# Low parts of two units on other engines, and routing work regrouped, in an attention and two-MoE kernel

## The chip, the cores and the metric

The kernel runs on one core of one Trainium2 chip, in one launch. The metric is the device time in microseconds (us), as a median of runs. A profiled execution gives the rows below; its times are us from the start of the span, unless they are marked ns. PE is the matrix engine (TensorE), PEld its weight loads, DVE is VectorE, ACT is ScalarE, POOL is GpSimd, SP is SyncE, which mostly issues DMAs (SPq and ACTq are DMA issues on those engines' queues).

## The reference, cut to what matters

```
def attn(q, k, v, centroids):          # B=2, H=8, S=768, D=64, 16 centroids a head
    q_assign = argmax(norm(q) @ norm(centroids).T); k_assign = the same of k
    scores = where(q_assign == k_assign, q @ k.T / sqrt(D), -1e9)
    return softmax(scores) @ v
def moe(x, w_gate, w1, w2, capacity):  # x 1536 x 512, 8 experts, hidden 1024, capacity 384
    e = argmax(x @ w_gate); gate = softmax(x @ w_gate)[e]
    keep the first `capacity` tokens of each expert, in order
    out[token] = gate * (relu(x @ w1[e]) @ w2[e])      # zero where not kept
def moe2(x, w_gate, w_output_gate, w1, w2):            # no capacity
    out[token] = gate * sigmoid(x @ w_output_gate)[e] * (relu(x @ w1[e]) @ w2[e])
return moe2(moe(attn(...)))
```

The output of the attention is the input of the first MoE (stage 1), whose output is the input of the second (stage 2). Each token has one expert per stage, so the rows of a stage are sorted by expert.

## The kernel before

**Attention.** The 16 heads of 768 rows are worked in 8 head pairs with 96 score tiles of 128 x 768 (`pss` L238, its row maximum `nm` L246 on DVE, exponential `pe` L254 on ACT, transposes `ppt` L268, product with v `av` L280). `norm` multiplies by the gate weights as well (`px` L299), so that the gate logits `lp` of stage 1 come with the output; `after_half` then chooses experts for each half (three tiles of 128 rows, C = 6 tiles in a batch of 768). At the start, centroids are loaded and normalised (`cl`, `cw` L355, `c_n` L66 to L68), logits against them give two masks of five steps each (`first_mask`, L207 to L217, to the transposes `poh` L223), and `first_rows(0)` builds the first operands. Matmuls on a zero tile (`keep_warm`, `warm_up`, L26) run in TensorE's idle time at the start.

**Experts.** A unit is a block of rows of one expert. Stage 1 has units 0 to 8 of 128, 64, 304, 208, 200, 192, 176, 168 and 120 rows, stage 2 has units 9 to 16 of 256, 136, 272, 120, 224, 128, 192, 160 and more; 0 and 9 are the heads, and open their expert without closing it. Every product is made of three f16 products of high and low parts. `mm1` works through eight f-steps of 12 matmuls (`ph` L930), after each of which ACT writes the high part `hh` (L932) and DVE the low part `hl` (L933). `mm2` follows with four d-steps (`py` L996, eight high, eight low-weight and eight `hl` matmuls each), or `pz` L971 by token, as in unit 9. `xg` is a block of gathered rows, transposed (`pxt` L907) and split into `xh` (ACT, L908) and `xl` (DVE, L909). Weights come as raw f32 by SP, and are split into `wh` (L820, ACT) and `wl` (L827, DVE) in half chunks.

**Handovers.** A stage's rows go to DRAM (x1d, x2d) once their experts and positions are known, and are read back by gathers on POOL (L867, `xg<-x2d,idx`), which need the indices `idx` from a DVE chain: choose the expert, count positions with a matmul (`ppos` L1522 in the attention, L1718 to L1721 in the second handover), scale the row (L1447 ACT, L1449 POOL; L1711 POOL), gates (L1753, L1755), invert the permutation (`av`, `rv` L587 to L595, matmul L600) and look up (L646, L649). At the end of stage 1 the outputs `yt` are first transposed back (`pyo` L1609), with logits `pq` (L1637, L1645; copy `lt` L1640) and a flag product (`flt`, `okr`, L1013, L1015), and scaled to `xo` (L1661, L1662). Groups of units (`group1`) are routed together.

**What sets the order.** Each engine's queue runs in program order, and waits on semaphores. `run()` writes the order by tables: `PIECES` gives a unit's weight splits per step, `SA` and `SB` the background steps per f- or d-step of the two heads (a background step is one `next` on the routing generators), `FX`, `FB`, `FY` the f-step at which the previous unit's `exit` starts. Where a routing generator yields, other work is placed. The last attention pair's second half, `last()`, is a background task of unit 0. The head's gather and entry stand as follows:

```
                if d == 1 and self.ngather == i + 2:
                    self.gather()
                if d == 3 and self.nmeta == i + 2:
                    self.meta()
            if head:
                assert nxt.gt, "unit not gathered"
                for k in range(len(nxt.tiles)):
                    self.entry(nxt, k)
```

## Time and profile before

| | before |
|---|---|
| median of 3 runs | 629.47 us (627.88 to 630.0) |
| the profiled execution | 627.58 us |
| its span | 625.7 us |
| mean granted TensorE clock | 0.976 |
| PE / PEld busy | 569.5 / 470.8 us |
| DVE / ACT / POOL busy | 467.1 / 419.9 / 212.8 us |
| DMA moved | 117.55 MB, mean 188 GB/s |

The profiled execution is 627.58 - 625.7 = 1.9 us longer than its span. A busy share says how much an engine worked, not that it set the end; the chain of waits and the idle time before an instruction say which engine another one waited for. The granted clock is the share of TensorE's full speed that it had: at 1.00 it ran at 2.4 GHz, at 0.50 at 1.2 GHz. In a timeline row the first number is the start, the second the length (of all of a row's instructions where it ends in x2 or more), and the brackets give the idle time of that engine ahead of the row and what ended it.

### The profile page before, as it was taken

The page shows a single profiled execution, that of the slowest core. Times are in us where ns is not written, and L with a number is a line of the kernel's source. Part 1 is how long each engine was busy: PE and PEld are TensorE (multiplying, and loading weights), DVE is VectorE, ACT ScalarE, POOL GpSimd, SP SyncE. Part 2 cuts the span into 40 slices and gives each one's busy share as a digit, 9 for nine tenths or more (in the row PEclk, how much of TensorE's full clock was granted, in tenths as well). Part 3 has the DMA queues.
Part 4 walks back from the last instruction along what each step waited for, and adds up shares of the span by engine and source line. Part 5 has one row for each costly group of instructions (what it writes and reads, how often), then busy time and mean ns, then how long its engine had stood idle before and what let it go on. Part 6 is the DMA issues. An engine that isn't in the chain of part 4 may idle for free.

```text
span 625.7 us, 14519 instructions
## 1 busy us (share of the span) xinstructions
PE 569.5 (91%) x5430; PEld 470.8 (75%) x5430; DVE 467.1 (75%) x1219; ACT 419.9 (67%) x885; POOL 212.8 (34%) x420
## 2 busy tenths in 40 slices
PE   6899999998999988958999998998788899999992
PEld 2766767675767666637878997997767888999992
DVE  5767777679899677756597689788776566989881
ACT  4766666776666669832676776876654466979781
POOL 8702020204150210134615268344333623253341
PEclk9899999999999999998899999999899799999998
DMA  5779391826429952314486776977754457998930
GB/s 148 212 231 275 97 216 46 210 60 151 141 89 233 252 171 82 133 56 138 130 269 204 243 244 179 304 238 244 248 181 152 164 174 238 305 308 298 321 111 20
DMA packets 75518, 117.55 MB, mean 188 GB/s; under 512 B 10504, under 2 KB 43400, under 8 KB 75441
## 3 DMA queue, kind: packets, MB, share of 16 engines
q1 hardware_dynamic: 71585, 105.96, 56.1%
q0 software_dynamic: 3264, 9.72, 4.9%
q8 instruction: 45, 0.74, 0.5%
q10 hardware_dynamic: 592, 0.87, 0.4%
q14 instruction: 32, 0.26, 0.1%
HBM read 84.28 MB, written 12.87 MB: 155 GB/s over the span
## 4 chain that ended last, share of the span: by engine, by line
PE 63%; DVE 16%; ACT 9%; DMA 5%; issue 4%; SPq 1%; POOL 0%; ACTq 0%; DVEq 0%; POOLq 0%
PE ph L930 17%; PE py L996 13%; PE av L280 9%; PE pss L238 7%; PE ppt L268 6%; DVE wl L827 3%; DVE nm L246 3%; PE pz L971 3%; ACT pe L254 2%; PE pyo L1609 2%; PE pxt L907 2%; ACT pt L270 1%; ACT wh L820 1%; DMA xg<-x2d,idx2a 1%; DMA xg<-x2d,idx 1%
## 5 line engine op out<-in xcount | busy, mean ns | idle before, releaser
L827 DVE SCALAR_TENSOR_TENSOR wl<-raw,sw,wh 128x1024 f16<-128x1024 f32 x128 | 163.5, 1283 | 18.5 <-ACT wh L820 18.4
L820 ACT ACTIVATE wh<-raw,sw 128x1024 f16<-128x1024 f32 x128 | 145.7, 1146 | 2.6 <-DMA x<-ot 2.5
L246 DVE TENSOR_REDUCE nm<-pss 128x1 f32<-128x768 f32 x96 | 91.4, 952 | 40.5 <-PE pss L238 36.8
L254 ACT ACTIVATE pe<-pss,nm 128x768 f32<-128x768 f32 x96 | 87.1, 907 | 24.2 <-DVE nm L246 24.2
L930 PEld LDWEIGHTS <-wh 128*128 128x128 f16 x1152 | 91.3, 102 | 14.2 <-issue 9.7
L238 PE MATMUL pss<-y,x 128*128 128x384 f32 x384 | 93.5, 364 | 4.1 <-ACT pe L254 3.2
L268 PE MATMUL ppt<-ident,pe 128*128 128x128 f32 x576 | 80.5, 275 | 3.3 <-ACT pt L270 1.4
L238 PEld LDWEIGHTS pss<-y,x 128*128 128x128 f32 x384 | 63.0, 190 | 24.4 <-issue 12.3
L270 ACT COPY pt<-ppt 128x384 f32<-128x384 f32 x128 | 57.9, 482 | 28.6 <-PE ppt L268 28.2
L268 PEld LDWEIGHTS ppt<-ident,pe 128*128 128x128 f32 x576 | 69.3, 142 | 8.9 <-ACT pt L270 2.3
L930 PE MATMUL ph<-xh,wh 128*128 128x192 f16 (+14 forms) x576 | 69.5, 246 | 6.7 <-DVE hl L933 5.7
L996 PEld LDWEIGHTS <-wh 128*128 128x128 f16 x960 | 72.4, 99 | 3.8 <-issue 0.5
L930 PE MATMUL ph<-xl,wh 128*128 128x192 f16 (+14 forms) x576 | 69.5, 246 | 0.2
L930 PE MATMUL ph<-xh,wl 128*128 128x192 f16 (+14 forms) x576 | 69.5, 246 | 0.0
L280 PE MATMUL av<-pt,v 128*64 128x384 f32 x384 | 68.8, 494 | 0.0
L932 ACT ACTIVATE hh<-ph 128x128 f16<-128x128 f32 (+14 forms) x144 | 44.1, 312 | 35.7 <-PE ph L930 34.3
L933 DVE SCALAR_TENSOR_TENSOR hl<-ph,hh 128x128 f16<-128x128 f32 (+14 forms) x144 | 46.4, 333 | 24.6 <-ACT hh L932 24.0
L930 PEld LDWEIGHTS <-wl 128*128 128x128 f16 x576 | 47.4, 102 | 1.9
L996 PE MATMUL py<-hl,wh 128*128 128x192 f16 (+13 forms) x480 | 46.6, 239 | 0.8 <-DVE hl L933 0.8
L996 PE MATMUL py<-hh,wh 128*128 128x192 f16 (+13 forms) x480 | 46.5, 239 | 0.6 <-DVE hl L933 0.4
L280 PEld LDWEIGHTS av<-pt,v 128*64 128x64 f32 x384 | 24.8, 136 | 28.4 <-issue 28.2
L996 PE MATMUL py<-hh,wl 128*128 128x192 f16 (+13 forms) x480 | 46.1, 239 | 0.0
(319 smaller groups left out, 858.8 us busy)
## 6 DMA issues: line engine op xcount, KB each, us to landing
raw<-in_moe_w SPq DMA_DIRECT2D x64, 1024.0 KB, 5.9
y<-kh SPq DMA_DIRECT2D x31, 192.0 KB, 4.0
x<-qh SPq DMA_DIRECT2D x30, 192.0 KB, 4.2
q<-in_q SPq DMA_DIRECT2D x8, 384.0 KB, 5.1
k<-in_k SPq DMA_DIRECT2D x8, 384.0 KB, 5.3
x<-ql SPq DMA_DIRECT2D x16, 192.0 KB, 3.6
v<-in_v SPq DMA_DIRECT2D x8, 384.0 KB, 4.1
out<-zt SPq DMA_DIRECT2D x1, 3072.0 KB, 11.0
```

The costliest lines, as they stand in the source:

```text
L238: nc.tensor.matmul(p[:, hf, :W], xx[:, c * P:(c + 1) * P], yy[:, hf * W:(hf + 1) * W], start=a, stop=o)
L246: nc.vector.tensor_reduce(nm, p[:, :, :W], axis=AX.XY, op=ALU.max, negate=True)
L254: nc.scalar.activation(pe, p[:, :, :W], AF.Exp, bias=d["nm", c, j], scale=1.0, accum_out=d["sm"][:, c, j:j + 1])
L268: nc.tensor.transpose(p[:, kc * P:(kc + 1) * P], pe[:, kh, kc * P:(kc + 1) * P], ident)
L270: eng(pt[:, kh * HALF:(kh + 1) * HALF, (c % HALF) * P:(c % HALF + 1) * P], p.rearrange("p (a b) -> p a b", a=HALF))
L280: nc.tensor.matmul(p[j * D:(j + 1) * D, :W], d["v"][:, j, kc, :], d["pt", hf, j][:, kc, :], start=(kc == 0), stop=(kc == C - 1))
L820: nc.scalar.activation(hi[:, :, s], x[:, :, s], AF.Copy, scale=sw)
L827: nc.vector.scalar_tensor_tensor(lo[:, :, s], x[:, :, s], sw, hi[:, :, s], op0=ALU.mult, op1=ALU.subtract, accum_out=fl)
L930: nc.tensor.matmul(p[:, :N], w[:, c, fs], x[:, c, :N], start=(k == 0), stop=(k == 11))
L932: nc.scalar.activation(hh[:, f, :N], p[:, :N], AF.Relu)
L933: nc.vector.scalar_tensor_tensor(hl[:, f, :N], p[:, :N], 0.0, hh[:, f, :N], op0=ALU.max, op1=ALU.subtract)
L996: nc.tensor.matmul(p[:, :N], w[:, f, s], x[:, f, :N], start=(k == 0), stop=(k == 23))
```

## The change

It does ten things. (1) `WARM` goes from 8 to 9 matmuls, `WARM2` from 6 to 10. (2) The centroids come by one DMA that writes both halves of the partitions, instead of two. (3) Three of mask 1's five steps are placed before `first_rows(0)`. (4) At the last attention pair, half 0's `after_half` runs at once when half 0 is done, and the sum's reciprocal of half 1 (`inverse`) is made there. (5) In the last half the exponentials, powers and counts go ahead of the positions matmul without yields between, and of the three row scalings of the last half one is ACT's, one POOL's and one DVE's (new). (6) In the head units 0 and 9 the low part is made by ACT, which writes the ReLU once more in f32 (`hr`, one buffer), and POOL, which subtracts the high part; DVE no longer does it. (7) `group1` routes unit 6 alone and 7 with 8, and `FB`, `FY`, `SA`, `SB`, `KL` and two rows of `PIECES` change. (8) The last copy of `yt` of stage 1 moves to ACT. (9) In unit 9 the next unit's entry transposes stand ahead of the last d-step. (10) Outside heads, gathers are issued up to one unit earlier. In a few routing generators a yield is left out for the last unit.

```
-WARM = 8
+WARM = 9
-WARM2 = 6
+WARM2 = 10
...
+        def inverse(pi, hf):
+            d = st[pi]
+            c0 = hf * HALF
+            ri = d["ri", hf] = end.tile([P, HALF, 2], F32, tag="ri", name="ri", bufs=2)
+            nc.vector.tensor_scalar_add(ri, d["sm"][:, c0:c0 + HALF, :], 1e-9)
+            nc.vector.reciprocal(ri, ri)
...
-                bg.extend([lambda: next(g, None)] * (24 if hf else 8))
+                if pi == NPR - 1:
+                    while bg:
+                        bg.pop(0)()
+                    for _ in g:
+                        pass
+                    inverse(pi, 1)
+                else:
+                    bg.extend([lambda: next(g, None)] * (24 if hf else 8))
...
-        for j in range(2):
-            nc.scalar.dma_start(cl[j * D:(j + 1) * D], centroids.rearrange("d (h j g) -> d h j g", j=2, g=G))
+        nc.scalar.dma_start(cl.rearrange("p h j g -> p (h j g)"),
+                            centroids.unsqueeze(0).to_broadcast([2, D, 2 * NP * G]))
...
-        for _ in masks[0]:
-            pass
+        for j, n in ((0, 5), (1, 3)):
+            for _ in range(n):
+                next(masks[j], None)
         keep_warm(WARM2)
         first_rows(0)
...
-    FB = 2
-    FY = 7
-    SA = (1, 0, 1, 0, 1, 1, 0, 1, 1, 0, 1, 1)
-    SB = (1, 3, 2, 1, 1, 1, 1, 1, 1, 1, 1, 1)
+    FB = 0
+    FY = 3
+    SA = (1, 1, 1, 0, 0, 1, 0, 0, 0, 0, 1, 1)
+    SB = (1, 1, 1, 1, 1, 1, 1, 1, 1, 1, 1, 1)
...
         nc.scalar.activation(hh[:, f, :N], p[:, :N], AF.Relu)
+        if u.opens and not u.closes:
+            hr = self.sm.tile([128, 256], F32, tag="hr", name="hr", bufs=1)
+            nc.scalar.activation(hr[:, :N], p[:, :N], AF.Relu)
+            nc.gpsimd.tensor_tensor(hl[:, f, :N], hr[:, :N], hh[:, f, :N], op=ALU.subtract)
+            return
         nc.vector.scalar_tensor_tensor(hl[:, f, :N], p[:, :N], 0.0, hh[:, f, :N],
                                        op0=ALU.max, op1=ALU.subtract)
...
+                if head and prev and d == 3:
+                    for k in range(len(nxt.tiles)):
+                        self.entry(nxt, k)
                 self.mm2(u, d)
...
-                if d == 1 and self.ngather == i + 2:
-                    self.gather()
+                if d == 1 and not head:
+                    for _ in range(i + 3 + (u.stage is not units[0].stage) - self.ngather):
+                        self.gather()
...
-group1=((0, 1), (2, 3), (4, 5), (6, 7), (8,))
+group1=((0, 1), (2, 3), (4, 5), (6,), (7, 8))
...
-                yield from turns_by(1000 if end else 3, R.choose(rp, lg, None, oh1[:, t], mx), sums())
+                yield from turns_by(2 if end else 3, R.choose(rp, lg, None, oh1[:, t], mx), sums())
...
                 if end:
+                    exps()
+                    turns(power(), before(), shift())
                     yield
                     pp = positions()
-                    exps()
-                    yield from turns_by(KS, before(), power(), shift())
                     for i in range(HALF):
                         scale(i)
-                    yield from turns_by(KS, places(), gates(), load_order())
+                    turns(places(), gates(), load_order())
+                    scale(HALF)
```

Three places of the program order, before and after. Ahead of the gathers of the second handover, on POOL (`xg` are the gathered rows, `idx` the table of row numbers, `g` the gates, 1711 and 1749 the row scalings), it was before:

```order
L1655 COPY xo<-xg 120x11
L1656 COPY tk_100<-xg 120x1
L1755 COPY xo<-g_7061 120x1
L1711 TENSOR_SCALAR xo<-xo,sx 120x512
L939 MEMSET ls_7188 128x8
L867 DMA xg<-x2d,idx_89 128x524
L867 DMA xg<-x2d,idx_89 8x524
L867 DMA xg<-x2d,idx_89 128x524 x2
L867 DMA xg<-x2d,idx_89 16x524
```

and with the change, on the same engine and at the same place, with the low parts `hl` of unit 9 (128 x 256) around them:

```order
L956 TENSOR_TENSOR hl<-hr,hh 128x256
L1794 COPY xo<-g_7029 128x1
L1794 COPY xo<-g_7029 40x1
L1794 COPY xo<-g_7029 120x1
L1749 TENSOR_SCALAR xo<-xo,sx 128x512
L1749 TENSOR_SCALAR xo<-xo,sx 40x512
L1749 TENSOR_SCALAR xo<-xo,sx 120x512
L956 TENSOR_TENSOR hl<-hr,hh 128x256 x4
L886 DMA xg<-x2d,idx_89 128x524
L886 DMA xg<-x2d,idx_89 8x524
L886 DMA xg<-x2d,idx_89 128x524 x2
L886 DMA xg<-x2d,idx_89 16x524
L956 TENSOR_TENSOR hl<-hr,hh 128x256
```

Three scalings instead of one stand ahead of the gathers, four low parts come between, and the eighth low part stands behind the five gathers.

On ACT, around the writes of the attention's last rows (`jk` are the squares' sums, `hh` the high parts of unit 0, `x1d` the DRAM tensor of rows), it was before:

```order
L1453 ACTIVATE sh<-sh 128x24
L932 ACTIVATE hh<-ph 128x128 x2
L1447 ACTIVATE x<-x,sx 128x512
L932 ACTIVATE hh<-ph 128x128 x4
L1467 DMA x1d<-x 128x524 x3
L998 COPY yt<-py 128x128 x3
```

and with the change:

```order
L955 ACTIVATE hr<-ph 128x128
L951 ACTIVATE hh<-ph 128x128
L955 ACTIVATE hr<-ph 128x128
L1478 ACTIVATE x<-x,sx 128x512
L1502 DMA x1d<-x 128x524 x3
L951 ACTIVATE hh<-ph 128x128
L955 ACTIVATE hr<-ph 128x128
L951 ACTIVATE hh<-ph 128x128
```

The three writes move from behind the eighth `hh` of unit 0 to behind the fifth, and each `hh` is followed by an `hr`.

On ACT in unit 8, the last one of stage 1, around the copy of the logits of 168 rows (`lt`; `hh` of 120 columns are unit 8's), it was before:

```order
L932 ACTIVATE hh<-ph 128x120
L820 ACTIVATE wh<-raw,sw_108 128x4x256
L932 ACTIVATE hh<-ph 128x120
L1640 COPY lt<-pq 128x168
L820 ACTIVATE wh<-raw,sw_108 128x4x256
L998 COPY yt<-py 128x120
```

and with the change:

```order
L839 ACTIVATE wh<-raw,sw_108 128x4x256
L951 ACTIVATE hh<-ph 128x120
L1676 COPY lt<-pq 128x168
L839 ACTIVATE wh<-raw,sw_108 128x4x256
L951 ACTIVATE hh<-ph 128x120
L927 CAST xh<-pxt 128x4x128
L951 ACTIVATE hh<-ph 128x120
```

The copy stood behind the eighth `hh` of unit 8 and now stands behind the fourth.

## Rows read from the trace of the kernel before

**Rows 1.** The page, parts 1 and 4: busy time, and the chain by engine.

```profile
PE 569.5 (91%) x5430; PEld 470.8 (75%) x5430; DVE 467.1 (75%) x1219; ACT 419.9 (67%) x885; POOL 212.8 (34%) x420
...
PE 63%; DVE 16%; ACT 9%; DMA 5%; issue 4%; SPq 1%; POOL 0%; ACTq 0%; DVEq 0%; POOLq 0%
```

**Rows 2.** Windows: length, busy PE, PEld, DVE, ACT, POOL, granted clock, DMA share, GB/s.

```profile
14.00:30.00 16.00, 13.55 (x80) 11.04 (x80) 12.62 (x22) 11.08 (x24) 12.87 (x62) 0.89 0.80 210
...
475.00:490.00 15.00, 10.05 (x85) 8.59 (x83) 6.79 (x21) 5.98 (x13) 9.13 (x19) 0.88 0.55 188
```

**Rows 3.** Windows: a stretch right behind the second handover, columns as above.

```profile
487.00:493.00 6.00, 5.64 (x47) 5.14 (x46) 2.59 (x6) 2.35 (x6) 5.08 (x16) 0.50 0.10 37
```

**Rows 4.** Timeline of the start: start, length, engine, line, operation, [idle before].

```profile
5.23 0.68 DVE L355 COPY cw<-cl 64x64 f32<-64x64 f32 x1 [0.89 <-DMA cl<-in_centroids]
...
9.28 1.47 PE L26 MATMUL warm<-wu 128*128 128x512 bf16 x6
...
12.04 0.81 PE L223 MATMUL poh<-ident,oh 128*64 128x128 f32 x6 [1.29 <-DVE oh L217]
...
13.12 1.02 DVE L227 TENSOR_SCALAR y<-poh 16x384 fp32r<-16x384 f32 x2 [1.22 <-ACT x L226]
...
17.68 0.82 PE L223 MATMUL poh<-ident,oh 128*64 128x128 f32 x6 [2.34 <-DVE oh L217]
```

**Rows 5.** Timeline of both handovers, of all engines.

```profile
274.79 1.00 PE L299 MATMUL px<-rw,avo 128*128 128x144 f32 x6 [0.58 <-ACT avo L287]
...
278.65 0.21 DVE L307 TENSOR_TENSOR lp<-px,ri 128x48 f32<-128x48 f32 x1
...
281.36 0.21 PE L1522 MATMUL ppos<-rs,to 128*128 128x8 f16 x2 [4.22 <-DVE rs L1529]
...
282.84 3.11 POOL L1449 TENSOR_SCALAR x<-x,sx 128x512 f32<-128x512 f32 x2 [1.32 <-DVE sx L671]
...
287.35 1.35 ACTq L1467 DMA_DIRECT2D x1d<-x  x3
...
290.89 0.18 DVE L649 TENSOR_REDUCE idx<-w 128x3 int32<-128x24 f32 x1
...
464.96 0.26 ACT L1640 COPY lt<-pq 128x120 f32<-128x120 f32 x1 [3.73 <-DVE okr L1015]
...
471.28 1.04 PE L971 MATMUL pz<-wh,hh 128*128 128x256 f16 x8
...
479.21 2.10 POOL L867 DMA_INDIRECT xg<-x2d,idx  x1 [3.99 <-DVE p2nov L663]
...
480.92 1.04 PE L971 MATMUL pz<-wh,hl 128*128 128x256 f16 x8
...
485.52 0.92 POOL L867 DMA_INDIRECT xg<-x2d,idx  x1 [0.30 <-issue]
...
486.54 1.64 PE L907 MATMUL pxt<-ident,xg 128*128 128x128 f32 x8 [4.59 <-DMA xg<-x2d,idx]
...
488.45 0.61 PE L930 MATMUL ph<-xh,wh 128*128 128x136 f16 x4 [0.27 <-ACT xh L908]
```

**Rows 6.** Timeline rows that give prices, of POOL, ACT and DVE.

```profile
12.25 1.81 POOL L128 TENSOR_TENSOR kl<-k,kh 128x768 fp32r<-128x768 f32 x1
...
458.61 0.36 ACT L932 ACTIVATE hh<-ph 128x256 f16<-128x256 f32 x1
...
459.05 3.13 POOL L1711 TENSOR_SCALAR xo<-xo,sx 128x512 f32<-128x512 f32 x4 [6.74 <-DVE sx L671]
...
471.00 1.28 DVE L827 SCALAR_TENSOR_TENSOR wl<-raw,sw,wh 128x1024 f16<-128x1024 f32 x1
```

**Rows 7.** Timeline of unit 8: POOL copies of one line beside a split.

```profile
450.73 0.20 POOL L1655 COPY xo<-xg 128x11 f32<-128x11 f32 x1
...
450.84 1.29 DVE L827 SCALAR_TENSOR_TENSOR wl<-raw,sw,wh 128x1024 f16<-128x1024 f32 x1 [0.21 <-ACT wh L820]
...
450.98 1.21 POOL L1655 COPY xo<-xg 40x11 f32<-40x11 f32 x1
```

More of the change, by code (lines that the diff above doesn't have):

```diff
@@ L299, in norm @@
                 nc.tensor.matmul(pv[:, c, :], ot[:, c * P:(c + 1) * P], rw[:, hp, :], start=True, stop=True)
-            ri = end.tile([P, HALF, 2], F32, tag="ri", name="ri", bufs=2)
-            nc.vector.tensor_scalar_add(ri, d["sm"][:, c0:c0 + HALF, :], 1e-9)
-            nc.vector.reciprocal(ri, ri)
+            if ("ri", hf) not in d:
+                inverse(pi, hf)
+            ri = d["ri", hf]
             rib = lambda n: ri.unsqueeze(3).to_broadcast([P, HALF, 2, n])
@@ L689, in __init__ @@
             u.opens = i == 0 or self.units[i - 1].j != u.j
+            u.ends = i + 1 == len(units)
         self.ranks = list(dict.fromkeys(u.j for u in self.units))
@@ L703, in __init__ @@
         self.last = False
+        self.ends = False
         self.xo = None
@@ L997, in mm2 @@
                 k += 1
-        (nc.vector.tensor_copy if d == 3 else nc.scalar.copy)(u.y[:, d, :N], p[:, :N])
+        (nc.vector.tensor_copy if d == 3 and (u.last or not u.ends) else nc.scalar.copy)(u.y[:, d, :N], p[:, :N])
         if u.last and d == 3:
@@ L1088, in run @@
                     self.limit += 1
-                if d == 1 and self.ngather == i + 2:
-                    self.gather()
+                if d == 1 and not head:
+                    for _ in range(i + 3 + (u.stage is not units[0].stage) - self.ngather):
+                        self.gather()
                 if d == 3 and self.nmeta == i + 2:
                     self.meta()
-            if head:
+            if head and not prev:
                 assert nxt.gt, "unit not gathered"
@@ L1102 @@
 KG = (4, 100, 5, 3, 0, 1)
-KL = 2
+KL = 4
 KC = (100, 3, 5, 4, 0, 1)
@@ L1278, in tile_kernel @@
                 prof1=(192, 304, 208, 200, 192, 176, 168, 120), prof2=(392, 272, 224, 192, 160, 128, 120, 88),
-                head1=128, head2=256, cut2=5, by_token=(0, 3, 5), group1=((0, 1), (2, 3), (4, 5), (6, 7), (8,)), seq1=(1, 2, 3, 4, 5, 6, 7), seq2=(1, 6, 2, 5, 3, 4, 7), dbg=None):
+                head1=128, head2=256, cut2=5, by_token=(0, 3, 5), group1=((0, 1), (2, 3), (4, 5), (6,), (7, 8)), seq1=(1, 2, 3, 4, 5, 6, 7), seq2=(1, 6, 2, 5, 3, 4, 7), dbg=None):
     nc = tc.nc
@@ L1447, in scale @@
                         nc.scalar.mul(x[:, i, :DM], x[:, i, :DM], sx[:, i:i + 1])
+                    elif end and i == HALF - 1:
+                        pass
+                    elif i == HALF:
+                        nc.vector.tensor_scalar_mul(x[:, i - 1, :DM], x[:, i - 1, :DM], sx[:, i - 1:i])
                     else:
@@ L1649, in exit1 @@
             ps = back(ys)
-            yield
+            if not unit.ends:
+                yield
             nc.gpsimd.tensor_copy(vb[:, k0:k1], unit.vb)
@@ L1702, in routed @@
             if last:
-                yield from rows
+                for _ in rows:
+                    pass
             next(gate)
@@ L1722, in routed @@
             lohi, ro = [], []
-            yield
+            if not last:
+                yield
             def places():
```

4 rows, old and new, of the table PIECES are left out of this document.

## The prediction

> **What bounds the kernel now.** I read the page first: TensorE is busy 91% of the span and the chain of waits that ended last runs 63% over it, with VectorE 16%, ScalarE 9% and DMA 5% [rows 1]. The windows by stage show where the other 9% lie: 14 to 30 us holds 13.55 of 16, 475 to 490 us 10.05 of 15 [rows 2]. So TensorE's gaps are what can be won here: the start, the handover from attention to the first experts (about 275 to 296 us) and the one from stage 1 to stage 2 (about 457 to 494 us). Each gap costs twice. In the stretch after the 4.59 us gap before 486.54 [rows 5] the granted clock was 0.50 of full speed, 1.2 instead of 2.4 GHz, although TensorE was busy 5.64 of 6 us [rows 3]; matmuls at half speed for 6 us are 3 us of work given away.
>
> **Baseline of the sum.** The profiled execution took 627.58 us, a span of 625.7 and 1.9 around it. The three runs have a median of 629.47, so I take the sum from 627.58 and add the 1.9 that the median lies above it. A measurement of this kernel can tell about 0.3%, 1.9 us, from no change.
>
> **A, the start: -1.6 us.** VectorE's second copy of the centroids, 0.68 us at 5.23, stood idle 0.89 us for the second of two loads [rows 4]. One load for both should land with the first; the idle and a little issue time go: -1.0. Next, TensorE waits 2.34 us before the one-hot transposes at 17.68 for the second mask's last operation [rows 4]. Three of that mask's five steps move ahead of `first_rows(0)`; what they give is bounded by the 1.22 us in which VectorE waited for ScalarE at 13.12 [rows 4] and which they can fill. But DMA is 0.80 busy from 14 to 30 us [rows 2], and pair 1 needs its loads there, so I count half, -0.6. Bounds: -1.0 (all of the second lost to the loads) and -2.2. The extra warm-up matmuls cost 0.245 us each (six took 1.47); four more make 1.0 us inside the 1.29 us gap before 12.04 [rows 4], and the ninth at the front stands where TensorE waits for the centroids. I count both at nothing; without that cover they would cost 1.4 at most.
>
> **B, the first handover: -2.1 us.** TensorE finished the last gate product at 274.79 + 1.00 = 275.79, yet VectorE began to use it (`lp`) only at 278.65, because the routing of half 0 and the reciprocals stood in front of it on VectorE [rows 5]. The change runs half 0's routing and both `inverse` steps while TensorE is still in `av`. So `lp` can start about 2.8 us earlier, and `ppos`, for which TensorE idled 4.22 us at 281.36 [rows 5], now stands after f4: that wait goes. What is late next is ScalarE. Its three `x1d` writes (1.35 us for the issue of all three, at 287.35 before [rows 5]) stood behind hh f7 and now stand ahead of hh f5. They wait for the scaled rows: 1.56 us for one Pool scaling (3.11 for two [rows 5]) and one on VectorE whose price no row shows. Its bounds are 0.36 us, an activation of half the columns [rows 6], and 1.56, Pool's for the same tile; I take 0.7, between VectorE's wl halved from 1024 to 512 columns (0.64) and the 0.78 that Pool needs for the same shape in stage 2 [rows 6]. They also wait for gates and codes behind it on VectorE. By that ScalarE stands until about 284 (an estimate: the old write time less 2.8, less the 0.7 saved on the last scaling). Then hh and hr of f5 to f7, six activations of at most 0.36 [rows 6], and hl f7 end at 286.6. A d-step of 128 rows costs 1.3, half of what 256 rows took (the first and the last of twelve groups of `pz` start at 471.28 and 480.92, so 0.876 each and three to a step [rows 5]); the first runs mostly before hl f7, the second ends at 288.0, and `pinv` behind it lets `idx` come at about 288.8 instead of 290.89 [rows 5]. Gathers and entry transposes follow: -2.1. Bounds: 0 (ScalarE's stall eats all) and -4.8 (2.8, and 2 of half-clock time after a shorter gap).
>
> **C, the second handover: +1.0 us.** Three things are added up.
> First, logits of the second-to-last stage-1 unit: `lt` on ScalarE waits for `okr`, which stands behind low-part work on VectorE; that wait was 3.73 us in unit 9 [rows 5] and I expect about as much in unit 8, ahead of hh f4. Unit 8's f7 then comes that much later, but the routing products that stood behind f7 (about 2.3 us, an estimate) now stand before it, so unit 9 starts some 1.4 us later.
> Second, gathers. Before, 14.25 us passed from `lt` of unit 8 at 464.96 to the first gather at 479.21 [rows 5]. Now that `lt` follows f0 of unit 9, whose hh came at 458.61 [rows 6]; 1.4 later and half a wl for `okr` put it at about 460.5. Of the 14.25 two wl of 1.28 [rows 6] and two low parts (0.7 together, at hh's price) leave VectorE's chain, and two more Pool scalings (0.78 each, from 3.13 for four [rows 6]) and their writes join it. The first gather starts near 460.5 + 14.25 - 2.6 - 0.7 + 1.9 = 473.3, about 6 us sooner; bounds 470 (scalings and low parts all hidden) and 475.7 (four low parts of f3 to f6 in front as well, at 0.6 each).
> Third, what the low parts cost on Pool. An hr on ScalarE repeats hh, 0.36 us at 256 columns. Pool's subtraction has no row; Pool's two-input `kl` took 1.81 us for 768 columns [rows 6], which gives 0.6 us for 256, an estimate. The eighth one, hl f7, is queued behind all five gathers. Those took from 479.21 to 485.52 + 0.92, 7.2 us [rows 5]. So hl f7 ends near 473.3 + 6.8 + 0.6 = 480.7, with TensorE waiting in d0 of the second product since about 474.8 (it ran from 471.28 before, is 1.4 later, and has two thirds of a step, 1.75, and some of the third that need no hl f7): an idle of 5.9 us where one of 4.59 was [rows 5]. Behind it come d1 and d2 (5.2 us), the transposes, now ahead of d3 (0.9, somewhat over half of the 1.64 at half clock), and d3 (2.6): unit 10 starts at 489.4, where it started at 488.45 [rows 5]. The wait is not removed but changed from a DMA to Pool. The half-clock stretch behind it [rows 3] stays. Bounds: -2.5 (gather at 470) and +5 (gather at 475.7, and Pool held by wl as below).
>
> **Pool beside wl.** A Pool copy of 40 x 11 took 1.21 us when a wl of 1.29 us had begun 0.14 us before it; the same line took 0.20 for 128 x 11 just before [rows 7]. The first gather took 2.10 us, the last 0.92 [rows 5]. So hl f7, if it meets one of the four wl that follow the routing, costs about 1.0 us more and C is +2; if none, +1. I take none, since wl also wait for ScalarE.
> The Trainium skill, page "SBUF — State Buffer", section "SBUF: two separate sides", says that VectorE with two SBUF inputs and GpSimd exclude each other on a shared port pair for a whole instruction. By that rule all four wl, 5.1 us, could stand before hl f7, and C would be +6; these two rows agree with the rule, and moving work to Pool is what it speaks against.
>
> **Sum.** -1.6 - 2.1 + 1.0 = -2.7: 627.58 becomes 624.9, and the median 629.47 becomes 626.8.
>
> **Rivals.** *The second handover works* (0.20). If Pool's low parts and scalings overlap the routing and gathers start at 470, TensorE's gap shrinks to some 2 us; the half-clock stretch of 6 us then goes too. That gives -2.5 - 3.0 for C, and -5.5 - 3.7 = -9.2: 620.3. For it: no wl and no hl is left in VectorE's chain there. Against it: hl f7 behind the gathers stays in any case.
> *Pool becomes the bound* (0.22, slower). hl f7 sits behind five gathers, and each hr has one buffer, so hr f waits for Pool's hl f-1. If gathers start at 475.7 and the train is held by two wl, hl f7 ends 2.4 + 2.2 + 1.0 later than I take it: C is +6.6, the sum +2.9, and with some of B lost to ScalarE +4: 633.5. It decides from a hl f7 that ends after about 484 (480.7 + 3.7, where C eats A and B and leaves none). For it: a Pool operation held by wl is seen in small [rows 7].
> *The moves find nothing* (0.11). Pair 1's loads set the start and the x1d writes set the first gather; Pool's wait equals the old one. Then 629.0, within 0.3%.
>
> **How the numbers follow.** My forecast has 0.47, with its own range 623.5 to 629.5; of it 0.33 lies below 627.6 (faster by over 0.3%) and 0.14 above. With the first rival's 0.20 and 0.02 of the third, faster is 0.55. Same takes 0.14 and 0.07, 0.21. Slower takes 0.22 and 0.02, 0.24. A range of 619.5 to 633.0 takes in the first rival and the near half of the second and leaves out under 2 in 10.
>
> **What the profile after would show.** A: the centroid copy without idle, poh(1) near 16 instead of 17.68. B: `lp` near 276, no PE wait at `ppos`, ACT idle before the x1d writes ending about 284, `idx` near 288.8. C: a wait of ScalarE at `lt` inside unit 8, the first stage-2 gather near 473, TensorE waiting about 6 us for Pool's hl in the second product of unit 9, and a half-clock stretch behind it; unit 10 starting close to 489 less what A and B gave. I am wrong if hl f7 is done before the second product needs it (then it is faster), if scalings and low parts push the gathers past 476, or if the clock stays up after the second handover.

## The result, and the profile after

The changed kernel took 636.44 us (median of 4 runs, 635.71 to 636.97) beside 629.55 us for the kernel before (4 runs): a ratio of 1.0114, with a 95% interval of 1.0092 to 1.0135. It is slower by 1.1%, some 7 us, where 626.8 us was forecast. The profiled execution's span is 634.9 us against 625.7, 9.2 us more.

The page of the changed kernel, busy time and chain, to be held against [rows 1]:

```profile
PE 574.0 (90%) x5435; PEld 470.5 (74%) x5435; DVE 466.3 (73%) x1202; ACT 423.6 (67%) x902; POOL 220.4 (35%) x435
...
PE 62%; DVE 14%; ACT 10%; DMA 5%; issue 5%; POOL 3%; SPq 0%; ACTq 0%; POOLq 0%; DVEq 0%
```

TensorE has the same work and five warm-up matmuls more; its 4.5 us more of busy time go with a mean granted clock of 0.969 where it was 0.976. Pool, which held nothing of the chain, now holds 3% of it.

A reader finds the place of a loss quickest by taking, in both timelines, the start of the same product of each unit and subtracting. These differences come from the first PE row of each product:

```
after minus before, us       start   difference   added in the step
first gate product (pair 0)  46.39 -> 49.38   +3.0   start +3.0
last gate product            274.79 -> 278.61 +3.8   attention +0.8
unit 2, ph 128x304           308.69 -> 312.60 +3.9   first handover +0.1
unit 8, ph 128x120           437.18 -> 442.44 +5.3   units 2 to 7 +1.4
unit 9, ph 128x256           455.52 -> 464.77 +9.3   unit 8 +4.0
unit 10, py 128x136          498.07 -> 507.23 +9.2   second handover -0.1
```

Two of these steps are not shown to be the change's. The start is taken up under a_start and b_start below. The +1.4 of units 2 to 7 lies in unit 5: behind a wait of 1.26 us that both profiles have, the granted clock was 0.50 from 390.8 to 394.2 in the changed kernel, and 1.00 from 381 to 400 before. The profile of b_start, which changes only the start, loses 1.3 us in unit 5 too, at half clock from 389.2 on; those of a_loads and a_whl9, which have the change's order there, do not have it.

The start, a timeline of the changed kernel (compare [rows 4]):

```profile
6.62 0.39 DVE L371 COPY cw<-cl 64x64 f32<-64x64 f32 x2 [5.33 <-DMA cl<-in_centroids]
...
11.28 4.31 PE L26 MATMUL warm<-wu 128*128 128x512 bf16 x10
...
15.42 0.82 PE L223 MATMUL poh<-ident,oh 128*64 128x128 f32 x6
```

The one load landed at 6.6 us, later than the second of the two (5.2). The ten warm-up matmuls ran at half clock, 0.43 us each (the granted clock was 0.50 from 8.5 to 15.3), and `poh` stood behind them. One step of mask 1 took 1.44 us, at 14.14.

The first handover (compare [rows 5]):

```profile
279.70 0.21 DVE L315 TENSOR_TENSOR lp<-px,ri 128x48 f32<-128x48 f32 x1 [0.51 <-PE px L307]
...
283.76 0.20 PE L1557 MATMUL ppos<-rs,to 128*128 128x8 f16 x2
...
286.00 1.99 POOL L1484 TENSOR_SCALAR x<-x,sx 128x512 f32<-128x512 f32 x1
286.15 2.68 ACTq L1502 DMA_DIRECT2D x1d<-x  x3
...
288.88 0.28 ACT L951 ACTIVATE hh<-ph 128x128 f16<-128x128 f32 x1 [2.75 <-DVE av L604]
```

`lp` came 0.1 us after the product where 2.9 us lay between them before, and `ppos` waits for nothing: the 4.22 us of [rows 5] are gone. But ScalarE stood at the three writes until 288.8, and TensorE waited 2.98 us at 289.37 for it. From 288.4 to 295.2 the granted clock was 0.50.

Unit 8 and the second handover (compare [rows 5] again):

```profile
444.73 2.32 POOL L1749 TENSOR_SCALAR xo<-xo,sx 128x512 f32<-128x512 f32 x2 [6.46 <-ACT z L569]
...
450.30 0.30 ACT L1676 COPY lt<-pq 128x168 f32<-128x168 f32 x1 [2.91 <-DVE okr L1040]
...
450.82 0.66 PE L926 MATMUL pxt<-ident,xg 128*128 128x128 f32 x4 [3.27 <-DMA xg<-x2d,idx2a]
...
460.10 0.21 PE L1021 MATMUL py<-hh,wh 128*128 128x120 f16 x1 [2.35 <-ACT hh L951]
...
482.27 1.11 POOL L886 DMA_INDIRECT xg<-x2d,idx  x1 [0.16 <-issue]
...
488.54 0.68 POOL L956 TENSOR_TENSOR hl<-hr,hh 128x256 f16<-128x256 f32 x1
...
489.28 0.39 PE L996 MATMUL pz<-wh,hl 128*128 128x256 f16 x1 [6.43 <-POOL vb L904]
```

In unit 8, two row scalings stand on Pool ahead of the gathers for unit 9's own rows, whose indices (`idx2a`) VectorE had ready at 441.11; these gathers began at 447.33, 4.9 us behind unit 8's first product, and TensorE waited 3.27 us for them. Before, they began 1.2 us ahead of that product (437.18), and TensorE waited 2.04 us:

```profile
435.94 1.11 POOL L867 DMA_INDIRECT xg<-x2d,idx2a  x1 [2.92 <-PE py L996]
```

TensorE then waited 0.42 and 2.35 us for hh f6 and f7, since ScalarE now scales unit 7's rows (L1698, L1699) ahead of them; before, that came behind unit 8's last hh. All of TensorE's waits in unit 8 over 0.4 us add up to 6.45 us, 3.18 before: 3.3 of the +4.0.

In the second handover the order is to be read off: five gathers from 482.27, then hl f7 at 488.54, then the one matmul of the second product that had waited 6.43 us for it. The releaser is printed as `vb`, the Pool instruction that came last by the profile; hl f7 ended just before. Behind it, windows of the changed kernel (columns as in [rows 2]) show half clock, as [rows 3] did:

```profile
487.00:493.00 6.00, 3.72 (x18) 2.67 (x19) 1.29 (x2) 1.60 (x3) 5.07 (x16) 0.50 0.32 96
```

### The profile page after: what moved, and what is told of

It reads as the page before. It is cut to its first block, busy times and chain, and to the rows that moved or that the text cites. A ratio compares the mean times of both kernels' runs of the same rounds, so it can differ in the third digit from the quotient of the medians.

```text
span 634.9 us, 14544 instructions
## 1 busy us (share of the span) xinstructions
PE 574.0 (90%) x5435; PEld 470.5 (74%) x5435; DVE 466.3 (73%) x1202; ACT 423.6 (67%) x902; POOL 220.4 (35%) x435
## 4 chain that ended last, share of the span: by engine, by line
PE 62%; DVE 14%; ACT 10%; DMA 5%; issue 5%; POOL 3%; SPq 0%; ACTq 0%; POOLq 0%; DVEq 0%
PE ph L949 15%; PE py L1021 14%; PE av L280 9%; PE pss L238 7%; PE ppt L268 5%; PE pz L996 3%; DVE nm L246 3%; DVE wl L846 2%; PE pyo L1645 2%; ACT pe L254 2%; PE pxt L926 2%; ACT pt L270 1%; ACT wh L839 1%; PE plog L153 1%; ACT qh L122 1%
## 5 line engine op out<-in xcount | busy, mean ns | idle before, releaser
L949 PE MATMUL ph<-xh,wh 128*128 128x192 f16 (+14 forms) x576 | 68.0, 242 | 8.2 <-DVE hl L958 4.8
L949 PE MATMUL ph<-xl,wh 128*128 128x192 f16 (+14 forms) x576 | 67.9, 241 | 0.2 <-issue 0.2
L949 PE MATMUL ph<-xh,wl 128*128 128x192 f16 (+14 forms) x576 | 67.9, 241 | 0.0
L958 DVE SCALAR_TENSOR_TENSOR hl<-ph,hh 128x192 f16<-128x192 f32 (+13 forms) x128 | 41.0, 332 | 22.8 <-ACT hh L951 22.2
L1021 PE MATMUL py<-hh,wh 128*128 128x192 f16 (+13 forms) x480 | 47.8, 242 | 6.8 <-ACT hh L951 3.3
L949 PEld LDWEIGHTS <-wl 128*128 128x128 f16 x576 | 46.0, 100 | 2.0
```

The costliest lines, as they stand in the source:

```text
L949: nc.tensor.matmul(p[:, :N], w[:, c, fs], x[:, c, :N], start=(k == 0), stop=(k == 11))
L958: nc.vector.scalar_tensor_tensor(hl[:, f, :N], p[:, :N], 0.0, hh[:, f, :N], op0=ALU.max, op1=ALU.subtract)
L1021: nc.tensor.matmul(p[:, :N], w[:, f, s], x[:, f, :N], start=(k == 0), stop=(k == 23))
```

## The experiments

Each kernel ran beside runs of the kernel before on the same chip, whose executions spread from 622.7 to 635.8 over all chips; so ratios are compared, each with its 95% interval, and a difference under 0.3% between two of them is not resolved. "+x at" a product is its start in a profile less that in the profile of before, as in the table. "a_" starts from the changed kernel, "b_" from the kernel before.

**Parts undone in the changed kernel.**

a_start: the three parts of the start as before; the centroid loads as in a_loads below, and

```
-WARM = 9
+WARM = 8
-WARM2 = 10
+WARM2 = 6
...
-        for j, n in ((0, 5), (1, 3)):
-            for _ in range(n):
-                next(masks[j], None)
+        for _ in masks[0]:
+            pass
```

> The changed kernel with the start undone: two centroid loads, 8 and 6 warm-up matmuls, the masks in the old order. Theory: the first gate product of the attention came 3.0 us later with the change and kept that delay through six pairs, so undoing the start gives 3.0 us, about 633.5 us, 0.6% above the kernel before. Rival: a later wait takes the gain back (loads of the next pairs, the first handover), less than 1 us.


Measured 636.42 us, ratio 1.0149 (1.0104 to 1.0195): nothing came back. The theory fell, and with it the reading of the start from one pair of profiles. This kernel's start has the same instructions as the kernel before, and still reached `poh` at 14.63 instead of 12.04 [rows 4]. Its timeline shows why:

```profile
6.95 0.83 PE L153 MATMUL plog<-q,cw 128*32 128x384 f32 x1
...
12.48 1.79 POOL L128 TENSOR_TENSOR kl<-k,kh 128x768 fp32r<-128x768 f32 x1
12.61 1.88 DVE L217 TENSOR_TENSOR oh<-eq,m 128x192 f32<-128x192 f32 x1
...
14.63 0.82 PE L223 MATMUL poh<-ident,oh 128*64 128x128 f32 x6 [2.37 <-DVE oh L217]
```

The logits took 0.83 us each, about as in the changed kernel where its granted clock was 0.50 (0.84); in the profile of before they took 0.49. So the mask came 1.1 us later, met Pool's 1.8 us subtraction, and its last step took 1.88 us instead of 0.39. Whether it does so differs between executions of the same start: of the four profiles with it, before's and b_hl's have 0.49 and reach the first gate product together, a_start's and b_half0's have 0.83 and reach it 2.7 and 3.3 us later. The profile of before fell on the good side.

a_loads: two centroid loads again.

```
-        nc.scalar.dma_start(cl.rearrange(...), centroids.unsqueeze(0).to_broadcast([2, D, 2 * NP * G]))
+        for j in range(2):
+            nc.scalar.dma_start(cl[j * D:(j + 1) * D], centroids.rearrange(...))
```

> The changed kernel with two centroid loads again, all else as changed. Theory 1: the single load that writes all 128 partitions lands 1.1 us later, and TensorE's longer idle time ahead of the first product is what precedes the fall of its clock to 0.50 between 8.4 and 15.2 us; with two loads both go and 3 us come back. Theory 2: the clock falls anyway, because the ten warm-up matmuls change nothing of it; then 1.1 us come back and the ten warm-up matmuls still take about 4.3 us.


Measured 635.26 us, ratio 1.0108 (1.0078 to 1.0139). The first product moved from 7.61 to 6.56, as both theories had it, and the first gate product stood at +1.0 instead of +3.0; the whole shows no difference that can be told from 1.0114. The ten warm-up matmuls took 2.33 us here, as at full clock, so theory 2 is wrong on that, and theory 1's 3 us are not in the median.

a_hl7: VectorE makes hl f7 of unit 9.

```
-        if u.opens and not u.closes:
+        if u.opens and not u.closes and (not u.stage is self.units[-1].stage or f < 7):
```

> The changed kernel, but the last low part (f7) of unit 9 made by VectorE as before, so that it is not queued behind the five gathers on Pool. Theory: TensorE's 6.43 us wait in the second product of unit 9 goes, unit 10 starts some 5 to 6 us earlier, and with the half-clock stretch behind the gap gone up to 8. Rival: the gathers themselves are what unit 10 waits for; then the wait moves to the entry transposes and 2 us or less are won.


Measured 631.89 us, ratio 1.0052 (1.0025 to 1.0079): 0.6% (3.9 us) better than the changed kernel by this one instruction; that is less than the theory's 5 to 8 us and more than the rival's 2. In its profile the wait is gone and unit 10's first product (`ph`, 488.45 before) starts at +5.7 instead of +11.6:

```profile
482.12 1.04 PE L996 MATMUL pz<-wh,hl 128*128 128x256 f16 x8
...
488.93 0.99 PE L926 MATMUL pxt<-ident,xg 128*128 128x128 f32 x8 [0.54 <-DMA xg<-x2d,idx]
...
494.19 0.40 PE L949 MATMUL ph<-xh,wh 128*128 128x136 f16 x4 [1.53 <-ACT xh L927]
```

From 480 to 500 us the granted clock was 1.00: with the gap gone, the half-clock stretch went too. The second handover, which came out even with before in the changed kernel (-0.1), is 5.2 us shorter than before here (+9.5 at unit 9, +4.3 at unit 10's `py`).

a_hl9: all low parts of unit 9 on VectorE.

```
-        if u.opens and not u.closes:
+        if u.opens and not u.closes and u.stage is self.units[0].stage:
```

> The changed kernel with all eight low parts of unit 9 made by VectorE as before; unit 0 as changed. Theory: it removes the wait for hl f7 as the run with f7 alone did (4.5 us), and also the 1.4 us for which TensorE waited on hr ahead of f7 and the four Pool subtractions ahead of the gathers, so about 6 us below the changed kernel, 1.003 to 1.005 of the kernel before. Rival: VectorE's routing chain, 3 us longer by the low parts, delays the gathers as much as Pool did; then it equals the run with f7 alone, 1.005, or is slower.


Measured 630.93 us, ratio 1.0032 (1.0000 to 1.0064): of the 1.14%, 0.8 are Pool's low parts in unit 9. The median fits the theory, but it is not resolved from a_hl7, and the interval holds the rival's 1.005 too.

a_hlno: the branch for `hr` never taken, so all low parts are VectorE's.

```
-        if u.opens and not u.closes:
+        if False:
```

> The changed kernel with the low parts of both heads on VectorE; no hr anywhere. Theory: in unit 0 ScalarE's second activation and the one hr buffer (hh, hr and Pool in turn, 0.82 us a step) hold TensorE by 0.66 and then, behind the row writes, 2.98 us; without them a further 1.5 to 3 us go against the run with only unit 9 on VectorE. Rival: the three row writes on ScalarE set the end of the first product either way; then 0.5 us or less.


Measured 631.14 us, ratio 1.0015 (0.9980 to 1.0050): under 0.3% against a_hl9, so the theory's 1.5 to 3 us are not shown. The wait ahead of the second product of unit 0 was 3.37 us, for VectorE's hl now, with hr gone. The rival is not excluded in size, but it named the row writes, and what came last here is VectorE.

a_group: the old grouping, piece tables and yields.

```
-              (1, 0, 0, 0, 0, 0, 0, 0, 1, 1, 1, 1),
-              (0, 0, 0, 0, 1, 0, 0, 0, 0, 1, 0, 1),
+              (0, 1, 0, 0, 0, 0, 0, 1, 0, 1, 0, 1),
+              (1, 0, 0, 0, 1, 0, 0, 0, 0, 1, 0, 1),
-    FB = 0
-    FY = 3
+    FB = 2
+    FY = 7
-    SB = (1, 1, 1, 1, 1, 1, 1, 1, 1, 1, 1, 1)
+    SB = (1, 3, 2, 1, 1, 1, 1, 1, 1, 1, 1, 1)
-KL = 4
+KL = 2
...
-            if not unit.ends:
-                yield
+            yield
-                for _ in rows:
-                    pass
+                yield from rows
```

`group1` ends in (6, 7), (8,) again, and the yield behind the positions matmuls is unconditional too. 

> The changed kernel with the grouping of the stage-1 outputs, the step tables of the stage-2 head and the yields as before (units 6 and 7 routed together, 8 alone), low parts still on Pool. Theory: the 4.0 us that unit 8 lost come back, but the gathers of the second handover start about 6 us later against unit 9 and hl f7 with them, so it is 2 to 3 us slower than the changed kernel. Rival: the regrouping cost only, and it is 4 us faster.


Measured 634.51 us, ratio 1.0103 (1.0069 to 1.0137). Neither: with the low parts on Pool the grouping changes nothing that can be resolved. In its profile, of the fastest of its runs, unit 8 took 2.1 us less than before (the changed kernel +4.0) and the second handover 2.9 us more (-0.1); the 3 us between these are not in the median.

a_gh: a_group's edits and a_hlno's, and the entry transposes where they were:

```
-                if head and prev and d == 3:
-                    for k in range(len(nxt.tiles)):
-                        self.entry(nxt, k)
-            if head and not prev:
+            if head:
```

> The changed kernel with the grouping, the step tables of the stage-2 head, the place of the entry transposes and all low parts as before; the start, the first handover's order, the gathers' places and the rest of the tables as changed. Theory: the regrouping and Pool's low parts are what costs, so about the kernel before, 0.998 to 1.002. Rival: the start and the places in the middle cost 2 us or more of themselves, then 1.004 or above.


Measured 628.88 us, ratio 1.0012 (0.9980 to 1.0044): the kernel before, as the theory had it. a_hlno, with the new grouping, has nearly the same ratio, so the regrouping is about even in itself if VectorE makes the low parts: in a_hlno's profile unit 8 lost 4.2 us and the second handover, with its earlier gathers, gave 5.8 back; in a_gh's they gave 1.3 and 0.5. A cost of up to 0.4% is not excluded: a_hlno's median is 2.3 us above a_gh's, and that of a_wno below is 2.8 us above a_wgh's, each beside the same runs of the kernel before.

**Parts alone in the kernel before.**

b_half0: half 0's routing run at once, and `inverse`.

```
-            ri = end.tile([P, HALF, 2], F32, tag="ri", name="ri", bufs=2)
-            nc.vector.tensor_scalar_add(ri, d["sm"][:, c0:c0 + HALF, :], 1e-9)
-            nc.vector.reciprocal(ri, ri)
+            if ("ri", hf) not in d:
+                inverse(pi, hf)
+            ri = d["ri", hf]
...
-                bg.extend([lambda: next(g, None)] * (24 if hf else 8))
+                if pi == NPR - 1:
+                    while bg:
+                        bg.pop(0)()
+                    for _ in g:
+                        pass
+                    inverse(pi, 1)
+                else:
+                    bg.extend([lambda: next(g, None)] * (24 if hf else 8))
```

> The kernel before with one part alone: the routing of half 0 and the reciprocals of half 1 run ahead of the last half's output product. Theory: the first gate use on VectorE moves from 278.65 to about 275.9, the 4.22 us wait of TensorE at the position matmul shrinks to about 1.5, and with ScalarE free of hr the gain is kept: 2 to 2.8 us faster, 0.996. Rival: the writes and the inverse permutation behind the second product's step d1 set the end of the handover: less than 0.5 us.


Measured 625.01 us (12 runs), ratio 0.9928 (0.9896 to 0.9959): more than the theory's 0.4%. In its profile `ppos` waits 1.45 us instead of 4.22 [rows 5], and the delay fell from +5.6 at the last gate product to -0.1 at unit 2. Part of that is clock: the profile of before had half clock for 3.4 and 6.8 us between 281 and 302 us, while this one stayed at 1.00 from 276.5 to 315 (its 3.4 us of half clock lie ahead of the last gate product, from 272.8, and are in the +5.6).

b_start: the three parts of the start. 

> The kernel before with the three parts of the start alone: one centroid load, mask 1's three steps ahead, 9 and 10 warm-up matmuls. Theory from the profiles: the single load lands 1.1 us later, and the earlier mask steps give most of that back, so within 0.3%, 0.999 to 1.003. Rival 1: as predicted, 1.6 us faster. Rival 2: as the profile of the changed kernel reads, 3 us slower.


Measured 629.60 us (12 runs), ratio 1.0030 (0.9998 to 1.0062): the theory, at its upper edge. The start does not help; the forecast's -1.6 lies outside the interval.

b_hl: only the `hr` branch.

```
+        if u.opens and not u.closes:
+            hr = self.sm.tile([128, 256], F32, tag="hr", name="hr", bufs=1)
+            nc.scalar.activation(hr[:, :N], p[:, :N], AF.Relu)
+            nc.gpsimd.tensor_tensor(hl[:, f, :N], hr[:, :N], hh[:, f, :N], op=ALU.subtract)
+            return
```

> The kernel before with only the heads' low parts moved to ScalarE and Pool. Here the gathers of the second handover stand behind hl f7, not ahead of it. Theory: the 6.4 us wait comes from Pool's low parts and the earlier gathers together, so without the regrouping the move costs little: 0 to 2 us in unit 0 (one hr buffer) and 0 to 1 in unit 9, 1.000 to 1.005. Rival: Pool is slow in itself, and unit 9 waits for it in each f-step; then 4 us or more, above 1.006.


Measured 632.90 us (10 runs), ratio 1.0082 (1.0049 to 1.0115). Worse than the theory, and by another way than the rival: most of the profile's loss is in unit 0, where the delay rose from 0.7 to 3.5 us. The profile is of its fastest run and shows 2.6 us in all, half of what the ratio says. Pool's queue there, a timeline of b_hl:

```profile
285.90 3.81 POOL L1455 TENSOR_SCALAR x<-x,sx 128x512 f32<-128x512 f32 x2
289.68 0.42 POOL L937 TENSOR_TENSOR hl<-hr,hh 128x128 f16<-128x128 f32 x1
```

Two scalings of the last half stand ahead of a low part; `hr` has one buffer, so ScalarE waited 3.38 us at 290.13 to overwrite it, and the next hh with it.

**The row writes.**

a_write: the writes move behind the yield that follows `inv`, with one more step in `SA`.

```
-                    for i in range(HALF):
-                        write(nc.scalar, slice(i, i + 1))
                     turns(taken())
...
                 yield
-                if not end:
-                    yield
+                if end:
+                    for i in range(HALF):
+                        write(nc.scalar, slice(i, i + 1))
+                yield
...
-    SA = (1, 1, 1, 0, 0, 1, 0, 0, 0, 0, 1, 1)
+    SA = (1, 1, 1, 0, 0, 1, 0, 0, 1, 0, 1, 1)
```

> The changed kernel with one move: the three row writes on ScalarE go from ahead of hh f5 to behind hh f7 of unit 0; low parts, groups and start as changed. Theory: the writes, which wait on ScalarE for the scaled rows and the gates, are what held hh f5 to f7, so TensorE's 2.98 us wait in the first product goes, and with it the clock's fall to 0.50 right behind it (6.8 us, 3.4 of work): 3 to 5 us below the changed kernel, 1.004 to 1.007 of the kernel before. Rival: hr and its one buffer hold ScalarE just as long; then 1 us or less.


Measured 635.32 us, ratio 1.0117 (1.0055 to 1.0180): no gain is shown in the whole, though the wide interval does not exclude the theory's upper half. In the profile the first handover did get 3.3 us shorter (+4.6 to +1.3), and unit 8 then lost 5.8 us instead of 4.0. TensorE's wait of 2.98 us became one of 1.86, in which `hr` waited 1.80 us for Pool's hl behind a row scaling: what is left is the rival's.

a_wgh: the same move in a_gh. 

> The changed kernel with the grouping, the place of the entry transposes and all low parts as before (1.001 of the kernel before when it was run so), and with the three row writes on ScalarE behind hh f7 of unit 0. Theory: the writes ahead of hh f5 are what takes half 0's gain back, so 0.5% comes back: 0.995 to 0.998. Rival: another part of the new order in the last half (the third row scaling on VectorE, the chain without yields) costs it; then 1.000 or above.


Measured 629.66 us (12 runs), ratio 0.9988 (0.9962 to 1.0013), not resolved from a_gh and between the theory and the rival. Its profile shows no shorter handover (+6.7 to +6.5), which is the rival's case. What ends TensorE's wait there is VectorE:

```profile
293.67 0.61 PE L1021 MATMUL py<-hh,wh 128*128 128x128 f16 x8 [3.38 <-DVE hl L958]
```

The change puts 27 routing operations on VectorE in one piece (288.38 to 293.41 here), and hl f5 to f7, if VectorE makes them, stand behind it.

a_wno: the move in a_hlno. 

> The changed kernel with the low parts of both heads on VectorE and the new grouping (1.0015 of the kernel before when it was run so), and with the three row writes behind hh f7 of unit 0. Theory: same gain as with the old grouping, 0.996 to 0.999. Rival: unit 8, which waits for gathers of its own under the new grouping, gives it back; then 1.001 again.


Measured 632.44 us (12 runs), ratio 1.0033 (1.0007 to 1.0060): as a_hlno, which is the rival's case; in its profile unit 8 lost 6.5 us.

a_whl9: the move in a_hl9, so that unit 0's low parts are on Pool and the writes late. 

> The changed kernel with unit 9's low parts on VectorE (1.003 of the kernel before when it was run so) and the three row writes behind hh f7; unit 0's low parts stay on ScalarE and Pool. Theory: ScalarE's writes and VectorE's uncut routing chain each hold unit 0, and only with low parts on Pool and writes late is neither in the way; the first handover gets 3 us shorter in the whole: 0.997 to 1.000. Rival: unit 8 or another wait gives it back: 1.002 or above.


Measured 629.79 us (12 runs), ratio 1.0000 (0.9979 to 1.0021). The median fits the theory, but the intervals of this and of a_hl9 (1.0032) overlap; the profile's first handover was 1.8 us shorter than before, and a_hl9's 1.2.

**Better versions.**

b_best: b_half0 with `WARM = 12`. 

> The kernel before with half 0's routing early (0.993 of the kernel before when it was run alone) and 12 instead of 8 warm-up matmuls at the front, which fill TensorE's idle time up to the centroid products. Theory: the logits at 7 us run at the full clock in more executions (0.49 us each instead of 0.83), and the first mask is then done ahead of Pool's 1.8 us subtraction; up to 2.9 us in such executions, 0.989 to 0.992. Rival: the clock at the start doesn't hang on them; then 0.993 again.


Measured 622.69 us (12 runs), ratio 0.9912 (0.9881 to 0.9943): faster than both kernels, and not resolved from b_half0's 0.9928. In its profile (618.4 us) the granted clock was 1.00 through the whole first handover, windows as in [rows 2]:

```profile
270.00:310.00 40.00, 33.52 (x511) 27.60 (x511) 27.84 (x120) 20.26 (x58) 24.49 (x40) 1.00 0.33 105
```

b_best2: b_best with mask 1's three steps ahead. 

> The kernel before with half 0's routing early, 12 warm-up matmuls at the front (0.991 when run so), and mask 1's three steps ahead of the first rows, two centroid loads as before. Theory: the three steps fill time in which VectorE waits, up to 1 us: 0.989 to 0.991. Rival: they push the second mask's work under Pool's 1.8 us subtraction, which holds VectorE, and nothing is won or up to 1 us lost: 0.991 to 0.993.


Measured 624.46 us (9 runs), ratio 0.9905 (0.9873 to 0.9937): the same. The mask order is worth nothing that these runs resolve.

## Why the prediction was wrong, step by step

**A, forecast -1.6.** The step that failed is "one load for both should land with the first". The single load, with 1.16 us of issue instead of 0.56, was there at 6.45 to 6.84 us in every profile with it, the second of two at 5.23 to 5.52. The mask steps gave nothing that b_best2 resolves. All three parts together measured +0.3% (-0.02 to +0.62). The warm-up matmuls, costed at nothing, cost nothing at full clock (2.33 us for ten, in a_hl7 and a_loads); in the first profile and in b_start's they ran at half clock, 4.3 and 4.45 us for ten, and stood in front of `poh`. The forecast's bound of 1.4 for five of them had only the full-clock price, by which it is 1.2. That `poh` loss of 3 us can't be put down to the change from one pair of profiles: a_start's, with the old start, has 2.6 of it by another way.

**B, forecast -2.1; +0.1 in the profile.** The mechanism was right and larger than forecast: half 0's early routing is worth 0.7% alone (b_half0), 4.5 us; in its profile the half clock behind the gap went too, which I had only in the bound. Two steps failed; both are counted here from the last gate product, which the changed kernel reached 3.8 us later. The first is "ScalarE stands until about 284", which is 9.2 us behind that product. It stood until 10.2 (288.8), 1.0 us longer, since Pool's scaling was queued behind hl f4 and took 1.99 us where 1.56 was taken (VectorE's own took 0.47, forecast 0.7, and was done at 287.51, earlier than Pool's); hl f7 ended at 13.3 instead of 11.8. The second is the d-step of 1.3 us, a price at full clock: at a granted clock of 0.50 the second d-step took 2.6. So `idx` came at 17.3, where 14.0 was forecast and 16.1 stood before.

Taking ScalarE's writes away is not enough: then Pool's scaling and the one `hr` buffer hold the low parts (a_write, 1.86 us), or VectorE's uncut chain does (a_wgh, 3.38 us). Between a_gh (1.0012) and b_half0 (0.9928), 0.8% are lost. Their profiles put that into the first handover: from the last gate product to unit 2 b_half0 took 5.7 us less than before, a_gh 0.3; behind unit 2 they differ by 1.1, up to unit 10. The start's 0.3%, within its interval, may have a part in it. The changed order in the last half has these two waits in it; how the loss divides between them is not settled.

**C, forecast +1.0; +3.9 in the profile (unit 8 +4.0, second handover -0.1).** The third item held: hl f7 was forecast to end 23.8 us after unit 9's first product and an idle of 5.9 us; it ended 24.4 us after it and the idle was 6.43. hl f6 met a wl and took 1.45 us, hl f7 met none and took 0.68, where 0.6 had been estimated. The forecast set this wait against the old one and called it nearly even, and so it came out. What it did not ask is what the earlier gathers are worth without this wait: a_hl7, a_hl9 and a_hlno have a second handover 5.2 to 5.8 us shorter than before, so one instruction at the end of Pool's queue took most of what the regrouping had to set against its loss in unit 8.

The term that I mis-sized is the first item, unit 8: +4.0 instead of +1.4. `lt` cost ScalarE 2.91 us (3.73 taken). I had not priced the two row scalings that now stand on Pool ahead of the gathers for unit 9's own rows (TensorE waited 3.27 us for these at 450.82, 2.04 before), nor the scalings of unit 7's rows that now stand on ScalarE ahead of unit 8's last two hh (2.77 us). Units 2 to 7, on which the prediction said nothing, lost 1.4 us in this profile by half clock that is not shown to be the change's.

**The rivals.** None of them is what happened. "Pool becomes the bound" has the direction, but not the way: it wanted gathers at 475.7 and hl f7 after 484. Counted from unit 9's first product, the first gather came at 17.5 us (16.4 forecast, 18.8 by the rival), and hl f7's end, put on the forecast's own clock, is 481.4, not 489; it was later only because unit 9 began 9.3 us later. The result lies above the rival's 633.5 because A gave nothing either and unit 8 lost more than any rival had. The chances had 0.24 on slower; the range ended at 633.0.

**The rule on the shared port.** It was right in a place where I had not looked. The Trainium skill, "SBUF — State Buffer", section "SBUF: two separate sides", has whichever of the two starts first hold the pair for its whole instruction, so it blocks in both directions. I priced Pool waiting for VectorE; a_start shows VectorE's mask step waiting for Pool's `kl` (1.88 us instead of 0.39), at the head of everything, which agrees with it.

## What to carry to other kernels

Price a moved instruction by what stands ahead of it in its new queue: a 0.68 us subtraction cost 0.6% of the kernel because five gathers stood in front of it and one matmul behind it waited. When a wait turns out no longer than the one it replaces, ask what the change would have won without it. Where a chain is made early (half 0's routing) check by itself that its gain survives; here it was worth 0.7%, and with the other parts of the same change nothing of it was left (a_gh). A difference of 3 us at the start between two profiles is not evidence while executions of the same start differ by as much: run the part alone, many times. Compare later stages from a product of their own, not by the clock of the span.

## What the runs showed of the hardware

- The same first instructions took either of two times in different executions: the centroid logits 0.49 us each in the profile of before and 0.83 in a_start's, with eight warm-up matmuls in both; in a_wno's and a_wgh's, with nine and on one chip, 0.49 (for the first six) and 0.83.
- A VectorE operation with two operands in SBUF took 1.88 us instead of 0.39 when a Pool subtraction of 1.79 us had begun 0.13 us ahead of it.
- One DMA that reads 32 KB twice to fill 128 partitions was there at 6.6 us; two that fill 64 partitions each were there by 4.2 and 5.2.
- Behind TensorE's 6.43 us wait in the changed kernel the granted clock was 0.50 from 487 to 493 us; in a_hl7, where the waits there were 0.54 and 1.53 us, it was 1.00 from 480 to 500. With short waits in the first handover (b_best) it stayed at 1.00 from 270 to 310 us.
